# Moving three kinds of side work in a fused attention, mixture-of-experts and SwiGLU kernel: weight conversion, the first expert's sums, and the last expert's down products

## The chip, the cores and the metric

The kernel runs on one core of a Trainium2 chip. A time is the device time of one execution in microseconds (us). TensorE does the matrix products, VectorE (DVE in the profile) and ScalarE (ACT) the elementwise work, GpSimd (POOL) a few small steps and the DMAs that add into memory; SyncE (SP) issues nearly all the other DMAs.

## The reference

Attention with two mask kinds gives x of 2304 tokens by 512. A mixture of eight experts follows, and then a SwiGLU layer:

```
logits = x @ w_gate;  P = exp(logits - max)          # 2304 x 8
8 times: P /= row sums + 1e-9; P /= column sums + 1e-9; P *= 2304 / 8
out = 0
for e in range(8):
    out += P[:, e:e+1] * (relu(x @ w1[e]) @ w2[e])    # 512 -> 1024 -> 512
xn = out / sqrt(mean(out * out) + 1e-6) * rms_g
g = xn @ w_gate2;  result = (g * sigmoid(g) * (xn @ w_val)) @ w_out   # 512 -> 1536 -> 512
```

The weights of the last layer arrive as 64-bit floats; everything else is computed in 32-bit floats, each product as three products of rounded high and low parts.

## The kernel before

The tokens are three blocks (qd 0, 1, 2) of 768. Attention and expert 0 come first (to 329.1 us). Experts 1 to 7 are then 42 **groups**: for each expert g two halves hh of its hidden units, and for each half the three blocks, forwards for hh 0 and backwards for hh 1. Products of 2 by 2 blocks are done with 7 multiplications instead of 8, so operands have to be combined by adds before and outcomes after. A group has 14 up products (`product`, L1217, 84 matmuls) and 14 down units (`unit`, L1816, 126 matmuls), the units 12 slots behind: most of a group's units run in the next group. Both stream 32,256 columns. The last layer is nine **passes**: three thirds p of its hidden units, each for the three blocks (2, 1, 0, then 0, 1, 2, then 2, 1, 0). A pass is two **rounds** j of 14 up products and, from the second round on, the 36 down matmuls of the round before. In this document a stretch of the trace that is called a group or a round is cut at every 84th matmul of L1217.

The order of everything on each engine is the order in which this program issues it. `bg` is a clock that advances by one *pump* (28 in a group, about 1.07 us each; 26 in a round of the last layer); side work hangs on it as steps with a lag in pumps. `Queue` runs its steps in order, one lag after the other; a queue that yields waits while a rough model has VectorE too far behind TensorE (`room`, used only when `tight`). `drain` issues what is left of something at once.

The side work that the change touches:

- **Conversion** (`convert`, L817 to L862): 72 items turn 64-bit weights into 32-bit ones. An item is one load into `cv`, seven VectorE instructions (`head` 2, `number` 2, `tail` 2, `whole` 1) on 256 columns, one store. There is one buffer: the next `head` waits for its load, and, as it overwrites `t`, for the store before. 40 items (and 8 `first_combos`, which make the first third's up weights in memory) go from group 5 to group 39, where what is left is issued at once; the other 32 go from pass 1 on, in the queue `conv`. `load_1` and `prepare_2`, which bring the last layer's weights for the next third, call `conv.drain`: they issue every item up to the one they need.
- **Second weights** (`second_weights`, L1090): at each half's first group (n divisible by 3) seven combined blocks of w2 are made, by subtractions (L1106), rounding on ScalarE (L1119) and remainders on VectorE (L1122), all on 256 columns.
- **Sums of the experts.** `evict_1` takes a unit's outcome from PSUM to `acc` (copy on ScalarE, L1837, or add on VectorE, L1848); `close_region` weighs it with the expert's probability on ScalarE (L1867) and adds it to the memory tile `y1d` by a POOL DMA (L1873). Expert 1's two halves are added in `acc` and closed once, after hh 1. Expert 0's sums lie unweighted in `y0d`; in groups 2 to 5 `first_sums` loads each of 18 tiles to `cv`, weighs it (L1942) and stores it to `y1d` as the start of the sum.
- **Into the last layer.** After group 41 the loop `PRE_UNITS` runs 8 of the 12 units that are left, and pass 0's first products are interleaved with the other 4. `turn_tile` transposes normalized tiles (L1467, L1468) and queues `norm_blocks`, which splits and combines them (L1484 to L1506) and stores them to `xnd`; blocks of `xnd` are the passes' x operands. Block 0's tiles are turned in round (0, 1) (`TURNS`), and its downs are held back for that. Steps of `norm_blocks` have lags of 2.5, 1.6 and 0.85 pumps for blocks 0, 1 and 2. The up weights of round (0, 1) are loaded from `w1d` by `ready_combos`, queued at steps 1 and 3 of round (0, 0).

Of the kernel before, what the change touches and what calls it, by code (L numbers as in the profile page):

```python
# [17 lines left out]
P = 128  # L18
# [62 lines left out]
class Queue:  # L81


    def __init__(self, clock, yields=False, limit=8):
        self.clock = clock
        self.yields = yields
        self.limit = limit
        self.items = []
        self.last = 0
        clock.queues.append(self)  # L90
# [23 lines left out]
def kernel(  # L114
# [751 lines left out]
    def conversion(items, wait):  # L866

        for n, (nm, f, half) in enumerate(items):
            load, head, number, tail, whole, store = convert(nm, f, half)
            tag = nm, f  # L870
            if n == 0:
                conv.add([(WRITE, load)], tag)
            conv.add([(wait, head), (STEP, number), (STEP, tail)], tag)
            if n + 1 < len(items):
                conv.add([(STEP, whole), (1, convert(*items[n + 1])[0]), (2, store)], tag)
            else:
                conv.add([(STEP, whole), (WRITE, store)], tag)
# [212 lines left out]
    def second_weights(g, hh, both=None):  # L1090

        if both is None:
            both = const.tile([P, 2048], F32, name="raw_2", tag="r")
        raw = [both[:, 1024 * r : 1024 * (r + 1)] for r in range(2)]
        b11, b12, b21, b22 = ([t[:, 256 * i : 256 * (i + 1)] for t in raw] for i in range(4))
        new = [fa[:, 4608 + 256 * r : 4864 + 256 * r] for r in range(2)]
        t1, t3, t2, t4 = new, b12, b11, b21

        def load(r):
            f = 2 * hh + r  # L1100
            for h in range(2):
                rows = w2[g][(f + h * (NF // 2)) * P : (f + h * (NF // 2) + 1) * P, :]
                nc.sync.dma_start(out=raw[r][:, 512 * h : 512 * (h + 1)], in_=rows)

        def sub(out, a, b):
            nc.vector.tensor_tensor(out=out, in0=a, in1=b, op=ALU.subtract)  # L1106

        def early(r):
            sub(t1[r], b12[r], b11[r])
            sub(t3[r], b22[r], b12[r])  # L1110
            return 600

        def late(r):
# [7 lines left out]
        def low(k, r):  # L1121
            nc.vector.tensor_tensor(  # L1122
                out=w2_piece(k, r, 1), in0=(b21, b11, t4, t2, t1, t3, b22)[k][r],
                in1=w2_piece(k, r, 0).bitcast(F32), op=ALU.subtract,
            )
            return 256

        def begin():
            prep2.add([(WRITE, lambda: load(0)), (0, lambda: load(1))])

        def product(k):
            steps = []
            if k == 0:
                steps += [(READ, lambda: early(0)), (STEP, lambda: early(1))]
            steps += [(1, lambda: [high(k, r) for r in range(2)].clear()), (1, lambda: sum(low(k, r) for r in range(2)))]
            if k == 1:
                steps += [(1, lambda: late(0)), (1, lambda: late(1))]
            prep2.add(steps, ("w2", g, hh, k))

        return begin, product  # L1140
# [386 lines left out]
    with tc.manual_schedule():  # L1527
# [188 lines left out]
        for idx in range(-LOOK, n1 - LOOK):  # L1716
# [8 lines left out]
            if u.f == 0:  # L1725
                if "x" not in u.cell:
                    fetch(u)
                if u.left:
                    bg.add(gate(u.t0, u.n, u.cell["x"]), 20)
                    if u.at:  # L1730
                        area = fa[:, :1280], fa[:, 1280:3328].bitcast(F32R)
                        steps = sums(0, us[0].cell["x"], *area) if u.at == 1 else []
                        steps += sums(u.at, u.cell["x"], *area)
                        bg.add(steps, 30 if u.at == 1 else SUMS, tag="sums")
# [90 lines left out]
        def evict_1(n, k):  # L1825
# [9 lines left out]
            if (hh == 0 or E_STD < g < E - 1) and k in (0, 2, 3, 4):  # L1835
# [20 lines left out]
            if (hh == (g < E - 1) or E_STD < g < E - 1) and k in (1, 5, 6):  # L1856
                close_region(g, qd, *((1, 0) if k == 1 else (0, None) if k == 5 else (1, 1)))
# [3 lines left out]
        def close_region(g, qd, half, col):  # L1861
# [71 lines left out]
        def first_sums(i):  # L1933

            qd, b = divmod(i, 6)
            buf = cv[:, 512 * (i % 2) : 512 * (i % 2 + 1)]

            def load():
                nc.sync.dma_start(out=buf, in_=y0d[:, tile_of(qd, b), :])

            def weigh():
                nc.scalar.activation(buf, buf, AF.Copy, scale=prob[:, tile_of(qd, b), 0:1])  # L1942

            def store():
                nc.sync.dma_start(out=y1d[:, qd, b // 3, b % 3], in_=buf)

            return load, weigh, store
# [16 lines left out]
        for n, (g, hh, qd) in enumerate(groups):  # L1964
# [12 lines left out]
            if n == 2:  # L1977
                steps = []
                for i in range(17, -1, -2):
                    l, w, t = zip(first_sums(i), first_sums(i - 1))  # L1980
                    steps += [*l, lambda: None, *w, *t]
                bg.add(steps, 62, tag="first")
# [74 lines left out]
        ])  # L2057
        def downs(r):
# [46 lines left out]
        for n, (p, qd) in enumerate(passes):  # L2105
# [10 lines left out]
            if n == 1:  # L2116
                conv.yields = False
                conversion(conv_items[40:], CONV_WAIT[1])
            for j in range(NG // 2):
# [14 lines left out]
                for ci, s in enumerate((2 * j, 2 * j + 1)):  # L2134
# [8 lines left out]
                    for i, (wk, xk, which, begins) in enumerate(PROD):  # L2143
                        fetch_left(None)
                        if n < NQD and j == 0 and ci == 0:
                            for x in PROD[i : i + 3]:
# [6 lines left out]
                        if first_round:  # L2153
# [15 lines left out]
                        if step in late:  # L2169
                            if NGP - 1 not in spares:  # L2170
                                spares[NGP - 1] = spare_of(NGP - 1)
                            turn_tile(groups[-1][2], late[step], db[late[step] % 3], spares[NGP - 1])
# [48 lines left out]
```

## Time and profile before

| | |
|---|---|
| median of 3 runs | 2202.3 us (2201.37 to 2205.28) |
| the profiled execution | 2203.58 us, span of its instructions 2201.8 us |
| TensorE busy | 2045.3 us, 93% |
| VectorE, ScalarE, GpSimd busy | 1622.5, 1300.6, 246.2 us |
| mean granted TensorE clock | 0.975 of full speed |

The profile has for each stretch the busy time of each engine, the granted clock and how busy the DMA engines are; for each engine, what ended its idle times; and the single instructions in order of time. Busy time is a union: two instructions that overlap count once, so a group's busy time can be less than its count times the mean.

### The profile page before, as it was taken

The page shows a single profiled execution, that of the slowest core. Times are in us where ns is not written, and L with a number is a line of the kernel's source. Part 1 is how long each engine was busy: PE and PEld are TensorE (multiplying, and loading weights), DVE is VectorE, ACT ScalarE, POOL GpSimd, SP SyncE. Part 2 cuts the span into 40 slices and gives each one's busy share as a digit, 9 for nine tenths or more (in the row PEclk, how much of TensorE's full clock was granted, in tenths as well). Part 3 has the DMA queues.
Part 4 walks back from the last instruction along what each step waited for, and adds up shares of the span by engine and source line. Part 5 has one row for each costly group of instructions (what it writes and reads, how often), then busy time and mean ns, then how long its engine had stood idle before and what let it go on. Part 6 is the DMA issues. An engine that isn't in the chain of part 4 may idle for free. (4 is left out here: it accounts for less than half of the span.)

```text
span 2201.8 us, 37643 instructions
## 1 busy us (share of the span) xinstructions
PE 2045.3 (93%) x13611; PEld 1938.0 (88%) x13611; DVE 1622.5 (74%) x3553; ACT 1300.6 (59%) x2991; POOL 246.2 (11%) x277
## 2 busy tenths in 40 slices
PE   8999998999999999999999999999987889894798
PEld 7788878989999999999999999999987778794697
DVE  4667657869787887878878788787886557675644
ACT  6756335756776777777777777777664334231222
POOL 6433200000111011110111111111000000000000
PEclk9999999999999999999999999999999999997899
DMA  6687675676877879778897887976757662432431
GB/s 184 162 234 190 201 244 202 213 256 152 240 198 191 243 174 263 193 208 239 218 279 208 234 212 185 265 191 183 221 151 262 229 200 82 151 131 79 135 143 58
DMA packets 357146, 429.54 MB, mean 195 GB/s; under 512 B 80800, under 2 KB 260192, under 8 KB 356960
## 3 DMA queue, kind: packets, MB, share of 16 engines
q1 hardware_dynamic: 321888, 368.20, 51.6%
q0 software_dynamic: 35072, 58.93, 16.0%
q8 instruction: 108, 1.77, 0.3%
q14 instruction: 78, 0.64, 0.1%
HBM read 301.75 MB, written 125.30 MB: 194 GB/s over the span
## 5 line engine op out<-in xcount | busy, mean ns | idle before, releaser
L1217 PE MATMUL ub<-xt,w1t 128*128 128x384 f32 x2328 | 477.7, 342 | 30.6 <-DMA xt<-xnd 14.5
L1217 PE MATMUL ub<-xx,w1t 128*128 128x384 f32 x1956 | 398.7, 341 | 47.0 <-DVE fa L1249 30.4
L1217 PEld LDWEIGHTS ub<-xt,w1t 128*128 128x128 f32 x2328 | 401.7, 192 | 41.0 <-issue 11.2
L1816 PE MATMUL db<-w2t,ht 128*128 128x256 f32 x2772 | 383.5, 283 | 8.9 <-DVE acc L1848 5.7
L1217 PEld LDWEIGHTS ub<-xx,w1t 128*128 128x128 f32 x1956 | 336.0, 191 | 55.7 <-DVE fa L1249 32.8
L1816 PEld LDWEIGHTS db<-w2t,ht 128*128 128x128 f32 x2772 | 369.1, 190 | 13.4 <-DVE acc L1848 9.5
L1816 PE MATMUL db<-w2t,hx 128*128 128x256 f32 x2520 | 350.9, 284 | 8.0 <-DVE acc L1848 3.8
L1816 PEld LDWEIGHTS db<-w2t,hx 128*128 128x128 f32 x2520 | 334.7, 190 | 17.7 <-DVE acc L1848 12.5
L1249 DVE TENSOR_TENSOR fa<-ub,fa 128x384 f32<-128x384 f32 x360 | 199.5, 554 | 180.2 <-PE ub L1217 171.3
L1368 ACT ACTIVATE fa<-fa 128x384 f32<-128x384 f32 x252 | 132.2, 525 | 192.9 <-DVE fa L1249 192.3
L1873 POOL DMA_DIRECT2D y1d<-acc x99 | 114.2, 1153 | 1097.1 <-ACT acc L1867 475.8
L1245 DVE TENSOR_TENSOR ht<-fa,ht 128x384 fp32r<-128x384 f32 x344 | 189.5, 552 | 45.0 <-ACT ht L1242 44.3
L1245 DVE TENSOR_TENSOR hx<-fa,hx 128x384 fp32r<-128x384 f32 x316 | 174.4, 552 | 35.9 <-ACT hx L1242 34.8
L1242 ACT ACTIVATE ht<-fa 128x384 fp32r<-128x384 f32 x344 | 177.2, 518 | 32.6 <-DVE fa L1420 32.2
L1242 ACT ACTIVATE hx<-fa 128x384 fp32r<-128x384 f32 x316 | 162.4, 520 | 56.7 <-DVE fa L1420 55.2
L1323 DVE TENSOR_TENSOR fa<-fa 128x384 f32<-128x384 f32 x336 | 185.5, 552 | 5.2 <-ACT fa L1364 0.7
L1867 ACT ACTIVATE acc<-acc,prob 128x256 f32<-128x256 f32 (+1 forms) x324 | 176.0, 572 | 16.2 <-DVE acc L1848 16.1
L1848 DVE TENSOR_TENSOR acc<-db,acc 128x768 f32<-128x768 f32 (+1 forms) x129 | 154.4, 1197 | 39.9 <-PE db L1816 38.9
L1360 ACT COPY fa<-ub 128x384 f32<-128x384 f32 x252 | 119.6, 475 | 107.0 <-PE ub L1217 103.4
L1385 ACT COPY fa<-ub 128x384 f32<-128x384 f32 x108 | 51.7, 479 | 129.8 <-PE ub L1217 129.6
L1837 ACT COPY acc<-db 128x768 f32<-128x768 f32 x144 | 115.1, 800 | 20.6 <-PE db L1816 16.4
L1403 ACT ACTIVATE fa<-fa 128x384 f32<-128x384 f32 x54 | 28.3, 525 | 110.1 <-DVE fa L1249 110.1
(259 smaller groups left out, 3145.3 us busy)
## 6 DMA issues: line engine op xcount, KB each, us to landing
xt<-xdt SPq DMA_DIRECT2D x111, 768.0 KB
xx<-xdt SPq DMA_DIRECT2D x92, 768.0 KB
y1d<-acc POOLq DMA_DIRECT2D x66, 384.0 KB, 7.3
y1d<-acc POOLq DMA_DIRECT2D x33, 768.0 KB, 10.1
xt<-xnd SPq DMA_DIRECT2D x25, 768.0 KB
xx<-xnd SPq DMA_DIRECT2D x24, 768.0 KB
fa<-in_moe_w_dram SPq DMA_DIRECT2D x56, 256.0 KB
raw<-in_moe_w_dram SPq DMA_DIRECT2D x52, 256.0 KB
```

The costliest lines, as they stand in the source:

```text
L1217: nc.tensor.matmul(ps[:, :TH], w[i][:, c], x[:, k, c], start=first and c == 0 and n == 0, stop=c == 1 and n == 2, skip_group_check=True,)
L1242: nc.scalar.activation(h[0], src, func)
L1245: engine.tensor_tensor(out=h[1], in0=src, in1=h[0].bitcast(F32), op=ALU.subtract)
L1249: nc.vector.tensor_tensor(out=out, in0=ps, in1=more, op=ALU.add)
L1323: nc.vector.tensor_tensor(**kw)
L1360: nc.scalar.copy(z[nm], ps)
L1368: nc.scalar.activation(z[nm], z[nm], AF.Relu)
L1816: nc.tensor.matmul(spot(k, m), hm[x], w[y], start=BEGIN[k] and r == 0 and m in FIRST[PAIR[k]] and i == 0, stop=r == 1 and i == 2, skip_gro ...
L1837: nc.scalar.copy(a, ps)
L1848: nc.vector.tensor_tensor(out=a, in0=ps, in1=a, op=ALU.add)
L1867: nc.scalar.activation(a, a, AF.Copy, scale=prob[:, tile_of(qd, b), g : g + 1])
L1873: nc.gpsimd.dma_start(out=y, in_=t, accum_op=ALU.add)
```

## The change

- `Queue` gets `paused`; `conv` is paused in the groups with n divisible by 3 up to group 38. Conversion starts at group 2 instead of 5, its wait before a `head` is 6 pumps instead of 11; `first_combos` waits 6 instead of 8.
- From pass 1 on (`quick`) the wait is 4 instead of 6, other steps have a lag of 1, and the next load and the store follow `whole` at once.
- `second_weights` works on 512 columns at a time: half the instructions.
- Expert 1 is closed after each half like experts 2 to 6. The closings of half 0 whose probabilities are not ready yet wait in a list until group 2; the first one of a place in `y1d` writes instead of adding. Expert 0's tiles are loaded in groups 7, 10, 13, 16 and 19 (four at a time), weighed 9 to 15 pumps later and added to `y1d` by POOL DMAs.
- `PRE_UNITS` is 12. Block 0's tiles are turned at steps 7 to 12 of round (0, 0); round (0, 1) has the common order of downs. Lags of `norm_blocks` are 1.0, 1.0, 0.85. The `w1d` loads for round (0, 1) are issued together, before pass 0, and the first load for the next third is queued there.
- The steps of one early `sums` task in expert 0 are spaced unevenly.

```diff
     def pump(self):
-        while self.items and self.last + self.items[0][1] < self.clock.now and (not self.yields or len(self.items) > self.limit or self.clock.room()):
+        while self.items and not self.paused and self.last + self.items[0][1] < self.clock.now and (not self.yields or len(self.items) > self.limit or self.clock.room()):
...
-    CONV_WAIT = (11, 6)
-    PRE_WAIT = 8
-    PRE_UNITS = 8
+    CONV_WAIT = (6, 4)
+    PRE_WAIT = 6
+    PRE_UNITS = 12
...
-    BLOCK_LAG = (2.5, 1.6, 0.85)
-    TURNS = (2, 3, 4, 6, 7, 8), (1, 1, 2, 2, 3, 3, 4, 5, 6, 6, 8, 9, 10, 12)
+    BLOCK_LAG = (1.0, 1.0, 0.85)
+    LAST_TURN = (7, 8, 9, 10, 11, 12)
+    Y0_AT = (7, 10, 13, 16, 19)
...
-    def conversion(items, wait):
+    def conversion(items, wait, quick=False):
...
-            conv.add([(wait, head), (STEP, number), (STEP, tail)], tag)
+            step = 1 if quick else STEP
+            conv.add([(wait, head), (step, number), (step, tail)], tag)
             if n + 1 < len(items):
-                conv.add([(STEP, whole), (1, convert(*items[n + 1])[0]), (2, store)], tag)
+                conv.add([(step, whole), (0 if quick else 1, convert(*items[n + 1])[0])], tag)
+                conv.add([(0 if quick else 2, store)], tag)
...
-        def high(k, r):
-            nc.scalar.activation(w2_piece(k, r, 0), (b21, b11, t4, t2, t1, t3, b22)[k][r], AF.Copy)
+        def place(k, s):
+            return w2t[:, k].rearrange("p s n -> p (s n)").rearrange("p (r s n) -> p r s n", r=2, s=2)[:, :, s]
+
+        def high(k):
+            nc.scalar.activation(place(k, 0), (b21, b11, t4, t2, t1, t3, b22)[k], AF.Copy)
...
-            if (hh == 0 or E_STD < g < E - 1) and k in (0, 2, 3, 4):
+            if (hh == 0 or g < E - 1) and k in (0, 2, 3, 4):
...
-                bg.drain("first")
-                if g < E - 1:
+                if (g, hh) == (E_STD, 0):
+                    nc.gpsimd.dma_start(out=y, in_=t)
+                elif g < E - 1:
                     nc.gpsimd.dma_start(out=y, in_=t, accum_op=ALU.add)
...
+        def first_sums(tiles):
+
+            t = const.tile([P, 2048], F32, name="y0_r", tag="r").rearrange("p (i n) -> p i n", n=DM)
...
+            for i, (qd, b) in enumerate(tiles):
+                bg.later(0, lambda i=i, qd=qd, b=b: load(i, qd, b))
+                bg.later(9 + 2 * i, lambda i=i, qd=qd, b=b: (weigh(i, qd, b), add(i, qd, b)))
...
             if n == 2:
...
+                waiting_for, early = early, None
+                bg.add([lambda a=a: close_region(*a) for a in waiting_for], 12, bg.now + 8)
+            if n in Y0_AT:
+                i = 4 * Y0_AT.index(n)
+                first_sums([divmod(x, 6) for x in range(i, min(i + 4, NTILE))])
...
-            if n == 5:
-                bg.drain("first")
+            conv.paused = n % NQD == 0 and n < NGP - 3
+            if n == 2:
                 conversion(conv_items[:24], CONV_WAIT[0])
...
+        prep.drain(("w1", E, 1))
+        for j in (2, 3):
+            for part in range(1, 5):
+                ready_combos(E, j, part)
+        prep.add([(WRITE, lambda: load_1(E + 1, 0))])
...
-                conversion(conv_items[40:], CONV_WAIT[1])
+                conversion(conv_items[40:], CONV_WAIT[1], True)
...
-                            for x in PROD[i : i + 3]:
+                            for x in PROD[i : i + 4]:
...
-                            if step == 1:
-                                prepare_1(E, 2)
-                            if step == 3:
-                                prepare_1(E, 3)
+                            if step in LAST_TURN:
+                                t = LAST_TURN.index(step)
+                                if t == 0:
+                                    spares[NGP - 1] = spare_of(NGP - 1)
+                                turn_tile(groups[-1][2], t, db[t % 3], spares[NGP - 1])
```

## Rows read from the trace of the kernel before

**Rows 1.** The page: engines; two groups of instructions (busy, mean ns | idle before, releaser)

```profile
PE 2045.3 (93%) x13611; PEld 1938.0 (88%) x13611; DVE 1622.5 (74%) x3553; ACT 1300.6 (59%) x2991; POOL 246.2 (11%) x277
...
L1867 ACT ACTIVATE acc<-acc,prob 128x256 f32<-128x256 f32 (+1 forms) x324 | 176.0, 572 | 16.2 <-DVE acc L1848 16.1
L1848 DVE TENSOR_TENSOR acc<-db,acc 128x768 f32<-128x768 f32 (+1 forms) x129 | 154.4, 1197 | 39.9 <-PE db L1816 38.9
```

**Rows 2.** Busy time by stretch: groups 1 to 6, 7 to 40, rounds to 55

```profile
core 0: us, PE busy (x) PEld busy (x) DVE busy (x) ACT busy (x) POOL busy (x), PEclk, DMA share, GB/s
...
358.40:558.90 200.50, 188.12 (x1271) 183.62 (x1270) 160.05 (x336) 126.73 (x274) 9.19 (x8) 0.97 0.67 205
558.90:1602.60 1043.70, 1023.24 (x7143) 1006.56 (x7142) 854.80 (x1820) 770.25 (x1675) 116.27 (x101) 1.00 0.81 218
1602.60:2090.30 487.70, 398.12 (x2036) 361.88 (x2035) 331.93 (x770) 179.11 (x396) 4.61 (x5) 0.92 0.48 156
```

**Rows 3.** Busy time by stretch: single groups 4, 5, 6, 12, 14, 20

```profile
454.10:491.10 37.00, 32.72 (x213) 31.99 (x212) 21.56 (x36) 21.41 (x45) 2.28 (x2) 0.91 0.74 235
491.10:521.00 29.90, 29.85 (x213) 29.53 (x211) 27.16 (x53) 19.02 (x43) 3.45 (x3) 1.00 0.76 189
521.00:558.90 37.90, 33.77 (x213) 32.65 (x212) 35.07 (x79) 23.38 (x57) 3.45 (x3) 0.91 0.67 170
711.00:744.70 33.70, 31.00 (x212) 29.83 (x211) 32.03 (x76) 25.83 (x61) 3.45 (x3) 1.00 0.87 245
774.60:804.90 30.30, 29.80 (x212) 29.48 (x211) 25.62 (x56) 21.92 (x47) 3.45 (x3) 1.00 0.63 150
959.60:989.40 29.80, 29.80 (x212) 29.48 (x211) 25.20 (x54) 21.93 (x47) 3.45 (x3) 1.00 0.65 155
```

**Rows 4.** What ScalarE waited for in 458 to 476 us

```profile
ACT cv L1942 <- DMA cv<-y0d: 4.0, 2, 2.6
```

**Rows 5.** VectorE's groups of instructions in group 12 (711.0 to 744.7)

```profile
L1122 DVE TENSOR_TENSOR w2t<-raw,w2t 128x256 fp32r<-128x256 f32 x12 | 4.5, 418 | 0.4 <-ACT w2t L1119 0.4
...
L852 DVE SCALAR_TENSOR_TENSOR cv<-cv 128x256 f32<-128x256 uint32 x2 | 0.8, 425 | 0.1
```

**Rows 6.** Busy time by stretch, from group 41 on

```profile
1602.60:1663.40 60.80, 48.17 (x325) 46.57 (x323) 51.49 (x118) 32.97 (x77) 2.91 (x3) 0.92 0.58 182
1663.40:1724.20 60.80, 50.78 (x273) 45.92 (x274) 39.60 (x83) 28.55 (x67) 1.71 (x2) 0.94 0.78 249
1724.20:1819.20 95.00, 77.53 (x361) 68.79 (x360) 55.30 (x133) 34.63 (x77) 0.00 (x0) 0.91 0.60 196
1819.20:1992.60 173.40, 165.28 (x842) 150.39 (x841) 125.38 (x292) 62.93 (x134) 0.00 (x0) 0.99 0.35 120
1992.60:2090.30 97.70, 56.36 (x241) 50.21 (x240) 60.16 (x147) 20.04 (x43) 0.00 (x0) 0.77 0.32 105
2090.30:2114.80 24.50, 23.29 (x121) 21.33 (x121) 12.78 (x24) 6.91 (x15) 0.00 (x0) 1.00 0.28 106
2114.80:2137.80 23.00, 23.00 (x122) 21.38 (x121) 10.40 (x20) 6.93 (x15) 0.00 (x0) 1.00 0.54 190
```

**Rows 7.** What TensorE waited for in the whole span: total, times, longest

```profile
PE ub L1217 <- DVE fa L1249: 43.2, 17, 26.2
PE ub L1217 <- DMA xt<-xnd: 14.5, 3, 5.2
...
PE ub L1217 <- DMA w2t<-w1d: 5.9, 1, 5.9
...
PE ub L1217 <- DMA xx<-xnd: 5.0, 1, 5.0
```

**Rows 8.** VectorE's groups of instructions in 1992.6 to 2057.4

```profile
L2097 DVE TENSOR_TENSOR acc<-db,acc 128x512 f32<-128x512 f32 x5 | 3.4, 685 | 2.0 <-PE db L729 1.9
...
L834 DVE TENSOR_SCALAR cv<-cv 128x256 uint32<-128x256 uint32 x8 | 2.3, 293 | 15.5 <-DMA cv<-in_moe_w_val_dram 7.9 <-DMA cv<-in_moe_w_out_dram 7.7
```

**Rows 9.** SyncE's queue in order of time, 1729 to 1745 and 1999 to 2006

```profile
1730.64 0.47 SPq L826 DMA_DIRECT2D cv<-in_moe_w_out_dram  x1
...
2001.96 0.38 SPq L829 DMA_DIRECT2D cv<-in_moe_w_val_dram  x1
```

**Rows 10.** VectorE in order of time, the same two stretches

```profile
1739.53 0.29 DVE L834 TENSOR_SCALAR cv<-cv 128x256 uint32<-128x256 uint32 x1 [7.82 <-DMA cv<-in_moe_w_out_dram]
...
1999.74 0.29 DVE L834 TENSOR_SCALAR cv<-cv 128x256 uint32<-128x256 uint32 x1 [2.50 <-DMA cv<-in_moe_w_val_dram]
...
2001.97 0.42 DVE L858 TENSOR_TENSOR cv<-cv 128x256 f32<-128x256 f32 x1
2005.00 0.29 DVE L834 TENSOR_SCALAR cv<-cv 128x256 uint32<-128x256 uint32 x1 [2.61 <-DMA cv<-in_moe_w_val_dram]
```

More of the change, by code (lines that the diff above doesn't have):

```diff
@@ L89, in __init__ @@
         self.last = 0
+        self.paused = False
         clock.queues.append(self)
@@ L1093, in second_weights @@
             both = const.tile([P, 2048], F32, name="raw_2", tag="r")
-        raw = [both[:, 1024 * r : 1024 * (r + 1)] for r in range(2)]
-        b11, b12, b21, b22 = ([t[:, 256 * i : 256 * (i + 1)] for t in raw] for i in range(4))
-        new = [fa[:, 4608 + 256 * r : 4864 + 256 * r] for r in range(2)]
+        raw = both.rearrange("p (r n) -> p r n", r=2)
+        b11, b12, b21, b22 = (raw[:, :, 256 * i : 256 * (i + 1)] for i in range(4))
+        new = fa[:, 4608:5120].rearrange("p (r n) -> p r n", r=2)
         t1, t3, t2, t4 = new, b12, b11, b21
@@ L1133, in product @@
             if k == 0:
-                steps += [(READ, lambda: early(0)), (STEP, lambda: early(1))]
-            steps += [(1, lambda: [high(k, r) for r in range(2)].clear()), (1, lambda: sum(low(k, r) for r in range(2)))]
+                steps += [(READ, lambda: sub(t1, b12, b11)), (STEP, lambda: sub(t3, b22, b12))]
+            steps += [(1, lambda: high(k)), (1, lambda: low(k))]
             if k == 1:
-                steps += [(1, lambda: late(0)), (1, lambda: late(1))]
+                steps += [(1, lambda: sub(t2, b22, t1)), (1, lambda: sub(t4, b21, t2))]
             prep2.add(steps, ("w2", g, hh, k))
@@ L1733 @@
                         steps += sums(u.at, u.cell["x"], *area)
-                        bg.add(steps, 30 if u.at == 1 else SUMS, tag="sums")
+                        if u.at == 1:
+                            bg.add(steps, 30, tag="sums", weights=[0.8] * 9 + [1.0] + [2.0] * 4 + [0.8] * 6)
+                        else:
+                            bg.add(steps, SUMS, tag="sums")
                 else:
@@ L1855, in evict_1, with close_region @@
                     prepare_2(E, (0, 2, 1, 3)[k - 3])
-            if (hh == (g < E - 1) or E_STD < g < E - 1) and k in (1, 5, 6):
-                close_region(g, qd, *((1, 0) if k == 1 else (0, None) if k == 5 else (1, 1)))
+            if (hh == 0 or g < E - 1) and k in (1, 5, 6):
+                args = (g, hh, qd) + ((1, 0) if k == 1 else (0, None) if k == 5 else (1, 1))
+                if early is None:
+                    close_region(*args)
+                else:
+                    early.append(args)
             if (g, hh) == (E - 1, 1) and k >= 5:
                 scales[k - 5].add(norm_scale(qd, 3 * (k - 5)), ("scale", qd))
-        def close_region(g, qd, half, col):
+        early = []
+        def close_region(g, hh, qd, half, col):
             part = slice(0, DM) if col is None else slice(256 * col, 256 * (col + 1))
@@ L1931, in second, with load, weigh, add @@
             tick()
[L1933 to L1947, printed above, removed]
+        def first_sums(tiles):
+            t = const.tile([P, 2048], F32, name="y0_r", tag="r").rearrange("p (i n) -> p i n", n=DM)
+            def load(i, qd, b):
+                nc.sync.dma_start(out=t[:, i], in_=y0d[:, tile_of(qd, b), :])
+            def weigh(i, qd, b):
+                nc.scalar.activation(t[:, i], t[:, i], AF.Copy, scale=prob[:, tile_of(qd, b), 0:1])
+            def add(i, qd, b):
+                nc.gpsimd.dma_start(out=y1d[:, qd, b // 3, b % 3], in_=t[:, i], accum_op=ALU.add)
+            for i, (qd, b) in enumerate(tiles):
+                bg.later(0, lambda i=i, qd=qd, b=b: load(i, qd, b))
+                bg.later(9 + 2 * i, lambda i=i, qd=qd, b=b: (weigh(i, qd, b), add(i, qd, b)))
         def next_blocks(slots, was):
```

34 lines of the change are left out of this document (7 added, 27 removed).

## The prediction, made before the change was run

> **What bounds the kernel now.** I read the page first, then the busy times by stretch, then what each engine waited for where a stretch was too long, and last the order of instructions at those places. The page says that TensorE is busy 93% of the span and VectorE 74% [rows 1]; a change that removes no matmul can win only TensorE's idle and half-clock time. The stretches say where that is. A group without loss takes 29.9 us, as the stretches at 491.1 and 959.6 do [rows 3]. Groups 1 to 6 take 200.5 where six such make 179.4: 21.1 lost. Groups 7 to 40 take 1043.7 against 34 x 29.9 = 1016.6: 27.1 lost. [...]
>
> The waits name the causes: VectorE late with L1249 (43.2 us, 26.2 in one piece), x blocks from `xnd` late (14.5 + 5.0), up weights from `w1d` late (5.9) [rows 7].
>
> **Groups 1 to 6.** In group 4 ScalarE stands 4.0 us for expert 0's tiles from memory [rows 4]; it is the engine that frees the up products' PSUM, TensorE stops behind it, and the group takes 37.0 at a clock of 0.91 [rows 3]. The change takes those loads out of groups 2 to 5. Group 6 takes 37.9 with VectorE busy 35.07: it makes second weights, converts, and adds expert 1's outcomes. Conversion is paused there, and 4 of 7 adds of a block (12 in all, 1.2 us each [rows 1]) become ScalarE copies; it falls under the 27.16 that group 5 bears without loss. What comes in: 9 more closings, 27 instructions of 0.57 us [rows 1] on ScalarE, most crowded in group 2, where the list is worked off; ScalarE is busy 126.7 of 200.5 [rows 2], so this is covered; without the cover it would cost its 15 us less the 18 weighings that leave. Nine POOL DMAs come too; POOL is busy for 11% of the span [rows 1], and nothing here waits on it. Conversion from group 2 adds some 5 us of VectorE work a group where there was none. Of the 21.1 lost, 7.1 (group 4) and 8.0 (group 6) go, 2 come back: 13 won; bounds 8 and 18.
>
> **Groups 7 to 40.** The loss sits in groups divisible by 3: group 12 takes 33.7 with VectorE busy 32.03, groups 14 and 20 take 30.3 and 29.8 with 25.62 and 25.20 [rows 3]. Of group 12's 32.0 two conversions go: seven instructions take from 1999.74 to 2002.39, 2.65 us, on an otherwise free VectorE [rows 10], so about 4.8 by two. The halved second weights: 12 remainders on 256 columns take 4.5, 0.375 each [rows 5], a 512-column instruction takes 0.685 [rows 8], so a pair saves 0.065 and 11 pairs 0.7. That leaves 26.5, between groups 14 and 5, and those lost 0.4 and nothing. [...]
>
> The paused conversion has to fit into two groups of three. An item's lags sum to 13.5 pumps instead of 18.5, so 28 / 13.5 = 2.1 items fall to each open group instead of 1.5, +1.5 us of VectorE work: about 27 in a group like 14 or 20, what group 5 bears. Counting pumps, the 40 items and 8 combos end within group 38 as before they ended within 38; no burst at 39. Expert 0's 18 tiles: loaded four at a time in a group's first pump, weighed 9 to 15 pumps (10 to 16 us) later, so a load may take the 8.9 us of the slowest row below; the 18 adds replace 18 stores and go through POOL. At nothing; if late, ScalarE stops as in group 4, at most 7 us for each of five. A conversion's load has 8 pumps, 8.6 us, instead of 14 until its `head`. It takes 3.0 (issue 2001.96, `head` 2005.00) on a free queue and 8.9 (1730.64 to 1739.53) behind x blocks [rows 9, 10], so a bad one costs 0.3 and its clearance is gone: I allow 5. Of 27.1 lost 14 are won; bounds 5 and 22.
>
> **From group 41 on**, by stretch [rows 6]. A clean round takes 23.0, or 24.5 where VectorE takes the outcome of a pass.
>
> *1602.6 to 1663.4, group 41 and 8 units.* VectorE is busy 51.5 of 60.8: it is the limit. Four units come in (29.9 / 28 = 1.07 us each, 4.3) with their outcomes and the first blocks of block 1's normalization, some 4 us more for VectorE. They cover the wait for the first x block that ends this stretch (one of the three on `xt`, 14.5 in all [rows 7]). 60.8 becomes 65; bounds 61 and 70.
>
> *1663.4 to 1724.2, pass 0.* It loses the four units and the 5.9 for `w1d`. VectorE's 39.6 lose the units' outcomes and gain block 0's turning and blocks from later: about 45 in 14.6 + 23 of matmuls. The 20 `w1d` loads now pass SP in a row, at 0.4 us each [rows 9] 8 us, and behind them wait the stores to `xnd`, whose buffers ScalarE refills: between 0 and 8, I take 3. 60.8 becomes 50; bounds 42 and 60.
>
> *1724.2 to 1819.2, three rounds.* They hold 15 us of the waits for `xnd` [rows 7], all but the one above, and slow clock behind them. Blocks 1 and 0 are now normalized a round or more earlier: 27 steps at 1.0 pump instead of 1.6 and 2.5. Clean: 70. *1819.2 to 1992.6, seven rounds* lose little now; clean is 5 x 23.0 + 2 x 24.5 = 164. *1992.6 to 2090.3, pass 6* takes 97.7 where 47.5 would be clean: conversion has fallen behind, the third third's weights drain it, and VectorE, through which every second product leaves PSUM, stands another 15.5 us for the loads [rows 8]. In quick form an item takes 7 pumps, 52 pumps a pass, so all 32 end in pass 5, and this goes to 49.
>
> The price lies in the rounds before. Per item VectorE's 2.65 us are only moved: the whole stretch has 331.9 busy [rows 2] and would have 413 to do it in. But a load now has 4 pumps, 3.5 us, until VectorE wants it. On a free queue 3.0 suffice. At 1730.64, behind x blocks, it took 8.9 and VectorE stood 7.82 [rows 9, 10]. A 5.4 us stop for each of the passes 1, 3 and 4, at whose ends x blocks are loaded, is 16: 75 for the three rounds (bounds 70 and 86), 174 for the seven (164 and 190).
>
> Sum: 65 + 50 + 75 + 174 + 49 = 413, 74.7 less than 487.7.
>
> **In all** 13 + 14 + 75 = 102 of the profiled execution's 2203.6, 1.3 above the median: 2100. The early `sums` steps are only respaced; 0, with 2 either way.
>
> **Rivals.**
>
> *A, the forecast,* 2100, 2075 to 2125: chance 0.55.
>
> *B, loads late.* VectorE stops at both loads that meet x blocks in a pass, and pass 0 has its 8 us behind SP: 16 + 5, and up to the same again from clock lost behind stops. 2125 to 2170, typically 2135; 0.2. [...] Against it: the DMA engines are 0.35 busy in the seven rounds [rows 6].
>
> *C, everything hides:* conversion's loads arrive in time and pass 0 runs at its matmuls' pace: 16 + 10 less, and middle losses at their lower bounds, 2045 to 2075; 0.17. Against it: VectorE at 85% in the first stretch.
>
> *D, slower.* Every quick load takes 8.9 us. Then 32 x 5.4 = 173 us of stops stand against 118 won without any; it decides from 3.7 us a stop, a mean latency of 7.2. The DMA share of 0.35 speaks against it, 0.60 in the three rounds for it. 2215 or more; 0.04.
>
> *E,* the conversion only moves VectorE's overload forward, so that pass 6's gain is lost in passes 1 to 4: 2150 to 2200; 0.04, half of it within 0.2% of before, which is about what a measurement of this kernel can tell from no change.
>
> Faster by over 0.2%: 0.94; within: 0.02; slower: 0.04. The range takes A, most of B and the upper part of C: 2064 to 2145.
>
> **What would show it.** Right: groups divisible by 3 at 30 to 30.5 us with VectorE near 27; no wait for `y0d` on ScalarE in groups 2 to 5; pass 6 under 52 us with no conversion in it; no wait for `xnd` over 1 us in passes 1 and 2. Wrong: VectorE idle at L834 for over 30 us in passes 1 to 5; pass 0 over 60 us; waits for `y0_r` on ScalarE in groups 7 to 19.

## The result, and the profile after

The changed kernel takes 2122.9 us (median of 4, 2121.6 to 2127.5) against 2201.8 (2199.3 to 2205.3): a ratio of 0.9644, 95% interval 0.9624 to 0.9664, so 79 us less. The forecast was 2100, in a range of 2064 to 2145. The profiled execution has a span of 2124.7 where before's had 2201.8. Every time and ratio here and below is of fast runs; one execution of the run e3_early, of 3260 us at a granted clock of 0.555, is left out. Cut at the same matmuls as before (us):

| stretch | before | forecast | after |
|---|---|---|---|
| start to group 1 | 358.4 | 358.4 | 352.4 |
| groups 1 to 6 | 200.5 | 187.5 | 185.2 |
| groups 7 to 40 | 1043.7 | 1029.7 | 1029.7 |
| group 41 and the units behind it | 60.8 | 65 | 62.7 |
| pass 0 (two rounds) | 60.8 | 50 | 72.1 |
| three rounds | 95.0 | 75 | 83.9 |
| seven rounds | 173.4 | 174 | 179.8 |
| pass 6 | 97.7 | 49 | 48.0 |
| the rest | 111.5 | 111.5 | 110.9 |

In the groups and in pass 6 the totals are near the forecast. Pass 0 is the miss: it was to get 11 shorter and got 11 longer.

First the busy times by stretch of the kernel after: groups 1 to 6, groups 7 to 40, and among them groups 4, 5, 6, 11 and 12, which answer to [rows 2, 3].

```profile
core 0: us, PE busy (x) PEld busy (x) DVE busy (x) ACT busy (x) POOL busy (x), PEclk, DMA share, GB/s
445.90:477.90 32.00, 30.14 (x213) 29.62 (x212) 21.72 (x48) 21.25 (x44) 3.02 (x3) 1.00 0.73 237
477.90:507.80 29.90, 29.90 (x213) 29.58 (x212) 25.93 (x58) 22.18 (x48) 3.45 (x3) 1.00 0.75 185
507.80:537.60 29.80, 29.80 (x211) 29.48 (x211) 27.50 (x52) 25.14 (x54) 3.48 (x3) 1.00 0.79 203
...
659.40:691.60 32.20, 30.45 (x212) 29.71 (x211) 25.44 (x56) 21.60 (x47) 3.45 (x3) 1.00 0.62 149
691.60:721.50 29.90, 29.90 (x213) 29.58 (x212) 27.65 (x52) 25.59 (x54) 3.45 (x3) 1.00 0.93 268
...
352.40:537.60 185.20, 180.80 (x1270) 178.04 (x1269) 154.74 (x327) 135.27 (x281) 15.57 (x17) 1.00 0.66 203
537.60:1567.30 1029.70, 1018.79 (x7143) 1005.58 (x7142) 836.19 (x1674) 774.24 (x1616) 131.97 (x119) 1.00 0.84 228
```

Groups 6 and 12 now hold VectorE at 27.5 and TensorE does not stop in them. Group 4 is 5 us shorter. Group 11 (659.4 to 691.6) is longer: it took 29.9 before, with VectorE busy 23.62. It is not alone. The eleven groups of this stretch that are divisible by 3 went from 352.6 to 329.5 in all, 23.1 won; the other 23 went from 691.1 to 700.2, 9.1 lost. What VectorE waited for at the two instructions of conversion's `head` in groups 7 to 40 (busy, mean ns | idle before, releaser), first in before, then in after:

```profile
L835 DVE TENSOR_SCALAR cv<-cv 128x256 f32<-128x256 f32 x37 | 10.9, 294 | 1.3
L834 DVE TENSOR_SCALAR cv<-cv 128x256 uint32<-128x256 uint32 x37 | 10.6, 286 | 1.4 <-DMA cv<-in_moe_w_gate_dram 1.4
```

```profile
L837 DVE TENSOR_SCALAR cv<-cv 128x256 f32<-128x256 f32 x33 | 9.7, 294 | 9.6 <-DMA m2g<-cv 7.2 <-DMA m2v<-cv 1.1 <-DMA m2o<-cv 0.3
L836 DVE TENSOR_SCALAR cv<-cv 128x256 uint32<-128x256 uint32 x33 | 9.6, 290 | 5.3 <-DMA cv<-in_moe_w_val_dram 2.5 <-DMA cv<-in_moe_w_out_dram 1.9 <-DMA cv<-in_moe_w_gate_dram 0.9
```

The first instruction waits for the item's load, 5.3 us instead of 1.4, and the second for the store of the item before, 9.6 instead of 1.3; in group 11 this is 3.2 us at one store. That these waits cost the other groups their 9.1 us is argued from the trace: no run gives the loads and stores there more time. Then the same view from group 41 on; it answers to [rows 6].

```profile
1567.30:1630.00 62.70, 54.70 (x369) 53.20 (x368) 55.82 (x127) 34.02 (x79) 2.91 (x3) 0.89 0.60 194
1630.00:1674.00 44.00, 22.45 (x110) 20.71 (x109) 21.64 (x48) 18.30 (x44) 1.70 (x2) 0.77 0.85 262
1674.00:1702.10 28.10, 24.45 (x123) 20.91 (x121) 20.81 (x48) 12.85 (x32) 0.00 (x0) 1.00 0.75 222
1702.10:1786.00 83.90, 75.64 (x360) 67.55 (x361) 57.32 (x143) 29.27 (x61) 0.00 (x0) 0.94 0.58 196
1786.00:1965.80 179.80, 167.94 (x842) 150.02 (x841) 142.60 (x344) 64.64 (x139) 0.00 (x0) 0.99 0.39 134
1965.80:2013.80 48.00, 46.19 (x241) 42.69 (x240) 32.33 (x65) 19.62 (x43) 0.00 (x0) 1.00 0.32 113
```

In the first round of pass 0 (second row) TensorE is busy for half of 44.0 us at a granted clock of 0.77, and VectorE and ScalarE are busy for half as well: no compute engine is the bound, something is waited for. What TensorE and then ScalarE waited for in that round (us in total, times, longest):

```profile
PE ub L1215 <- DVE fa L1404: 14.0, 1, 14.0
PE ub L1215 <- ACT fa L1383: 5.5, 1, 5.5
```

```profile
ACT acc L1482 <- DMA xnd<-acc: 12.8, 1, 12.8
ACT w2t L1083 <- PE ub L1215: 6.1, 1, 6.1
```

And SP's order of issue there (start, us):

```profile
1618.94 1.09 SPq L1080 DMA_DIRECT2D fa<-m2o  x1
...
1633.67 0.33 SPq L1080 DMA_DIRECT2D fa<-m2o  x1
1634.06 8.24 SPq L938 DMA_DIRECT2D w1t<-w1d  x16
...
1646.51 2.20 SPq L938 DMA_DIRECT2D last_r<-w1d  x1
...
1653.89 0.90 SPq L938 DMA_DIRECT2D w2t<-w1d  x2
1654.90 1.73 SPq L1516 DMA_DIRECT2D xnd<-acc  x3
```

Read backwards from the 14.0: TensorE waits for VectorE's `L1404`, which stands behind a remainder of the normalization (`L1483`), which waits for ScalarE's rounding (`L1482`), which waits for its buffer, which the stores to `xnd` at 1654.90 have to empty. Those stores stand on SP behind not 20 but 36 loads of `w1d`, which hold SP from 1634.06 until the first of these stores at 1654.90: 20.8 us. The first 16 are those of regions 0 and 1, put into a paced queue in group 41 and forced out by the `prep.drain` that the change added; ahead of them stands the second `m2o` load, which waits for its buffer until 1633.67. The first `m2o` load, issued at 1618.94 behind seven x blocks, lets ScalarE's `L1083` start only at 1632.29; that is the 5.5. (The row above names TensorE as what ended ScalarE's wait. The traces of e2_pool and e3_early name the load, and e5_m2o, below, settles it.)

### The profile page after: what moved, and what is told of

Its sections match the earlier page's. It is cut to its first block, busy times and chain, and to the rows that moved or that the text cites. A ratio compares the mean times of both kernels' runs of the same rounds, so it can differ in the third digit from the quotient of the medians.

```text
span 2124.7 us, 37479 instructions
## 1 busy us (share of the span) xinstructions
PE 2027.7 (95%) x13611; PEld 1926.7 (91%) x13611; DVE 1594.4 (75%) x3387; ACT 1312.5 (62%) x2932; POOL 268.4 (13%) x304
## 5 line engine op out<-in xcount | busy, mean ns | idle before, releaser
L1366 ACT ACTIVATE fa<-fa 128x384 f32<-128x384 f32 x252 | 132.3, 525 | 180.6 <-DVE fa L1247 180.3
L1240 ACT ACTIVATE ht<-fa 128x384 fp32r<-128x384 f32 x344 | 177.4, 518 | 37.9 <-DVE fa L1418 37.4
L1874 ACT ACTIVATE acc<-acc,prob 128x256 f32<-128x256 f32 (+1 forms) x351 | 190.8, 573 | 14.3 <-DVE acc L1849 14.0
L1849 DVE TENSOR_TENSOR acc<-db,acc 128x768 f32<-128x768 f32 (+1 forms) x117 | 143.0, 1222 | 33.3 <-PE db L1817 32.1
L1838 ACT COPY acc<-db 128x768 f32<-128x768 f32 x156 | 124.5, 798 | 19.8 <-PE db L1817 16.8
L1383 ACT COPY fa<-ub 128x384 f32<-128x384 f32 x108 | 51.4, 477 | 92.0 <-PE ub L1215 91.8
L981 DVE TENSOR_TENSOR w1t<-fa,w1t 128x256 fp32r<-128x256 f32 (+1 forms) x160 | 83.4, 525 | 11.1 <-ACT w1t L978 10.7
```

The source lines that it names most:

```text
L1240: nc.scalar.activation(h[0], src, func)
L1366: nc.scalar.activation(z[nm], z[nm], AF.Relu)
L1838: nc.scalar.copy(a, ps)
L1849: nc.vector.tensor_tensor(out=a, in0=ps, in1=a, op=ALU.add)
L1874: nc.scalar.activation(a, a, AF.Copy, scale=prob[:, tile_of(qd, b), g : g + 1])
```

## The experiments

All edits begin from the changed kernel. Ratios are to the kernel before on the same chip. For pass 0 the theory, T, is that SP's order makes it long; its rivals are V, VectorE's normalization work, and D, the bytes on the DMA engines.

### The loads' place: e1_spread, e2_pool, e3_early

e1_spread:

```diff
-        prep.drain(("w1", E, 1))
-        for j in (2, 3):
-            for part in range(1, 5):
-                ready_combos(E, j, part)
-        prep.add([(WRITE, lambda: load_1(E + 1, 0))])
...
+                            if step in (1, 3):
+                                prepare_1(E, 2 + step // 2)
```

> One part of the change is undone in the changed kernel: the 20 w1d loads for regions 2 and 3 go back into the paced queue at steps 1 and 3 of the first round; all else stays. Theory T (SP's order: 36 loads in a row keep the xnd stores waiting for 12.9 us, and so ScalarE, VectorE and TensorE): the stores of the last six tiles issue behind 16 loads instead of 36, some 11 us earlier; TensorE's 14.0 us gap at L1215 shrinks to 0-5, the first round falls from 44 to 30-36, the time from 2123 to 2107-2114. Rival V (VectorE's work of pass 0, six norm turns and their blocks beside a round, is the bound): the first round stays over 40, the time within 4 of 2123. Rival D (the loads' bytes on the DMA engines, not their issue): the stores issue early but land as late as before, gain under 5.

e2_pool:

```diff
-                nc.sync.dma_start(
+                (nc.gpsimd if j > 1 else nc.sync).dma_start(
                     out=at(7 * i + k, n).bitcast(F32).rearrange("p (k m) -> p k m", k=n),
```

> The 20 w1d loads for regions 2 and 3 are issued at the same place in the program, but by GpSimd instead of SP; all else as in the changed kernel. T: as the loads no longer stand ahead of the stores on SP, the stores issue some 11 us earlier; 14.0 us gap to 0-6, time 2107-2115. D (bytes on the DMA engines): the loads move just as many bytes at the same time, so the xnd stores and the x loads behind them land late all the same; gap over 9, time 2118-2124. V: within 4 of 2123.

e3_early:

```diff
                         prepare_1(*nxt, PARTS_AT[i])
+                        if n + 1 == NGP:
+                            prep.drain(("w1", E, r))
```

> The w1d loads for regions 0 and 1 (20) are issued in group 41 right behind the product that ends their region's use, not from a queue that yields to VectorE; so 16 of them no longer stand behind the second m2o load and ahead of the 20 loads and the stores. All else as in the changed kernel. T: the xnd stores issue some 8 us earlier, the 14.0 us gap falls to 4-8, and the 5.5 us gap at the start of the round, in which the product waits, goes if it is the w1d loads and stays if it is ScalarE's wait for the m2o load; time 2107-2116. V: within 4 of 2123.

Ratios 0.9641 (0.9614 to 0.9668), 0.9654 (0.9638 to 0.9670) and 0.9648 (0.9615 to 0.9680). None differs from 0.9644 by what the intervals can tell, so I read the traces by round. The two rounds of pass 0 in e1_spread, in e2_pool, and in e3_early:

```profile
1633.70:1664.00 30.30, 21.02 (x111) 18.45 (x110) 21.58 (x48) 18.18 (x44) 1.70 (x2) 0.89 0.95 291
1664.00:1699.40 35.40, 28.16 (x122) 24.23 (x121) 21.32 (x48) 12.99 (x32) 0.00 (x0) 0.87 0.92 286
```

```profile
1630.00:1672.30 42.30, 24.42 (x111) 22.40 (x110) 21.65 (x48) 18.41 (x44) 12.51 (x22) 0.76 0.88 289
1672.30:1700.60 28.30, 24.40 (x122) 20.87 (x120) 20.83 (x48) 12.89 (x32) 0.00 (x0) 1.00 0.74 220
```

```profile
1626.80:1663.10 36.30, 23.56 (x110) 21.83 (x109) 21.65 (x48) 18.30 (x44) 1.70 (x2) 0.76 0.87 264
1663.10:1691.00 27.90, 24.45 (x122) 20.91 (x121) 20.84 (x48) 12.90 (x32) 0.00 (x0) 1.00 0.76 226
```

V falls: the first round can take 30.3 with the same VectorE work (21.6). T is half right. In e1_spread the 14.0 us wait is gone and the first round is 13.7 shorter, but the second takes 7.3 more, with the DMA engines at 0.92. In e3_early the wait falls to 4.1 and pass 0 from 72.1 to 64.2; but this edit moves the bytes of 16 loads out of the round as well as their place on SP, and does not tell T from D. e2_pool does, in part. Its first round starts at 1630.0 as after's does. The stores issue on SP at 1644.77, ten us earlier, and ScalarE goes on at 1653.33 instead of 1658.80: 5.5 of the ten us reach it. So SP's order is part of the wait, and D fits the rest: with GpSimd issuing the loads, the stores had an earlier start, and half of it was lost again, in a round with the DMA engines 0.88 busy. TensorE still stops 6.7 and 6.6, and the round gains only 1.7, but this edit has a price of its own: GpSimd's step of the normalization (`L1455`) now stands behind the 20 loads. What ScalarE waited for in that round of e2_pool:

```profile
ACT acc L1482 <- DMA xnd<-acc: 5.6, 1, 5.6
...
ACT acc L1458 <- POOL cv L1455: 3.0, 1, 3.0
```

### Both together, and the m2o load: e4_both, e5_m2o, e6_all

e4_both is e1_spread with e3_early. e5_m2o is e3_early and

```diff
-        prep2.add([(WRITE, load), (READ, high), (STEP, low)], ("w2", i))
+        prep2.add([(WRITE, load), (14 if (g, f) == (E, 0) else READ, high), (STEP, low)], ("w2", i))
```

e6_all is all three.

> Both of the earlier edits in the changed kernel: the w1d loads of regions 0 and 1 issue in group 41 (as in e3_early), those of regions 2 and 3 go back into the paced queue of the first round (as in e1_spread). In single executions e3_early won 8 us over pass 0's two rounds (72.1 to 64.2), e1_spread 6 (the first round 44.0 to 30.3, the second 28.1 to 35.4). If SP's order alone held pass 0 (T), both add up: first round 28-31, second 28-31, pass 0 56-62, time 2107-2113. If the DMA engines' bytes hold it (D; they are 0.85 to 0.95 busy in all first rounds so far), the second edit only shifts the loads from the first round to the second: pass 0 63-66, time as e3_early or 1-2 more.

> e3_early, and ScalarE's first copy of the m2o weights comes 14 pumps after its load instead of 7. In after and e3_early ScalarE stands some 6 to 7 us at that copy, as the load lands 13 us after its issue behind seven x loads, and TensorE's 5.5 to 6.6 us gap at L1215 <- ACT L1383 follows. If that copy is the cause, the gap falls under 2 and pass 0 from 64 to 57-60, time 5-7 under e3_early's. Rival: the product waits for its x block or w1t in any case, the gap moves to another releaser and the time is within 2 of e3_early's.

> e4_both and e5_m2o's later copy together. T: first round near 25, second near 30, time 2102-2109. D: as e5_m2o within 2.

Ratios 0.9638 (0.9614 to 0.9662), 0.9604 (0.9582 to 0.9626), 0.9613 (0.9592 to 0.9635); medians 2122.9, 2112.6, 2117.1. Pass 0 in e4_both, in e5_m2o, and in e6_all:

```profile
1632.30:1663.20 30.90, 20.63 (x110) 18.52 (x109) 21.58 (x48) 18.19 (x44) 1.70 (x2) 0.89 0.79 235
1663.20:1696.80 33.60, 27.45 (x122) 23.20 (x120) 20.79 (x48) 12.89 (x32) 0.00 (x0) 0.90 0.87 269
```

```profile
1626.40:1658.50 32.10, 21.75 (x110) 19.52 (x109) 20.93 (x47) 17.10 (x41) 1.70 (x2) 0.84 0.93 294
1658.50:1687.10 28.60, 25.80 (x123) 22.55 (x121) 20.78 (x48) 13.01 (x32) 0.00 (x0) 0.94 0.73 217
```

```profile
1635.50:1661.30 25.80, 20.42 (x110) 18.33 (x109) 20.84 (x47) 17.03 (x41) 1.70 (x2) 0.93 0.89 269
1661.30:1696.30 35.00, 27.30 (x123) 23.61 (x121) 20.84 (x48) 12.98 (x32) 0.00 (x0) 0.90 0.83 257
```

Pass 0 takes 64.5, 60.7 and 60.8. Spreading the loads adds nothing once the first 16 are early (64.5 against e3_early's 64.2, 60.8 against 60.7): it gives time to the first round and takes it from the second, as D has it. It is no proof of D: in the second round SP issues nine of the spread loads right ahead of stores (1676.70 to 1681.85 in e1_spread), so that T could do the same. T's forecast for e6_all, 2102 to 2109, did not come. The later copy of `m2o` takes the wait at `L1383` from 6.6 to 2.1 and 3.5 off pass 0. So the changed kernel's pass 0 was 72.1 through the place of the first 16 loads (8) and the `m2o` copy (3.5); at 60.7 it is back to what it took before. These are single executions, but others agree: the five runs u1 to u5 below leave pass 0 alone and have it at 72 to 75, and e8_wait5, which has e5_m2o's edits, at 59. e5_m2o is faster than the changed kernel: the ratios differ by 0.0040, about 9 us, with about 0.0030 for the uncertainty of that difference.

What holds it at 60 is argued only. Pass 0 of e5_m2o moves 32.1 x 294 + 28.6 x 217 = 15.6 MB; at the higher of the two rates, at which the DMA engines are 0.93 busy, that is 53 us. No run took bytes away.

### The last layer's conversion: u1_plain, e8_wait5

u1_plain:

```diff
-                conversion(conv_items[40:], CONV_WAIT[1], True)
+                conversion(conv_items[40:], 6)
```

> The quick conversion of the last 24 half pieces is undone in the changed kernel: pace 6 and step 1.5 as before, pieces in their old order of issue; the conversion again ends in pass 6. Prediction's term: pass 6 goes from 48 back to 97 (+49), passes 1 to 5 lose their conversion stops (some 16 us by the prediction; 20 us of VectorE idle time at conversion loads in the trace of after, most of it hidden): time 2123+30 to 2123+45 = 2153-2168. Rival E (overload only moved forward): under +15.

Ratio 0.9831 (0.9811 to 0.9851), 2164.6: the quick form is worth 41 us. Its stretches: the three rounds, the seven, and pass 6.

```profile
1704.10:1782.60 78.50, 72.52 (x360) 65.14 (x361) 47.61 (x112) 30.29 (x64) 0.00 (x0) 0.98 0.52 183
1782.60:1955.80 173.20, 164.79 (x841) 150.46 (x840) 125.58 (x291) 63.90 (x136) 0.00 (x0) 0.99 0.36 121
1955.80:2053.40 97.60, 56.61 (x241) 50.71 (x240) 60.57 (x149) 19.74 (x43) 0.00 (x0) 0.77 0.33 107
```

Pass 6 is as before, 97.6 against 48.0: 49.6 won there, 5.4 and 6.6 paid in the rounds ahead. The prediction paid 16. The prediction's rival E, that what pass 6 gains is lost again ahead of it, is out.

e8_wait5 is e5_m2o with `CONV_WAIT = (6, 5)` in place of `(6, 4)`.

> e5_m2o (2112.6) with the last layer's conversion at a pace of 5 pumps instead of 4 until a piece's first step. u1_plain shows that quick conversion costs rounds 44 to 53 some 12 us. If these are waits for the pieces' loads, as the prediction has them (4 pumps, 3.5 us, against loads of 3.0 to 8.9), one pump more saves 3 to 7: 2106-2110. If it is VectorE's work that delays the outcomes, nothing changes: 2111-2114. If the conversion then ends too late for the last third's weights, pass 6 is over 50 and the time over 2115.

Ratio 0.9619 (0.9602 to 0.9635), median 2111.7: no different from e5_m2o's 0.9604. By stretch its trace is 5.0 and 3.4 shorter in the ten rounds (80.2 for 85.2, 177.3 for 180.7), as the loads theory asks, and pass 6 stays at 48.2; but up to group 41 that execution was 8.7 longer than e5_m2o's, in places that the edit does not touch. The median lies where the expectation had put VectorE's work as the cause (2111 to 2114), not where it had put the loads (2106 to 2110). VectorE's idle time at `L836` falls only from 19.0 to 16.1. That one pump more helps the rounds is shown in one trace, not in the time.

### One part undone: u5_weights, u2_pairs, u3_nopause, u4_adds

u5_weights takes `weights=[0.8] * 9 + [1.0] + [2.0] * 4 + [0.8] * 6` out of the first sums.

> One part undone in the changed kernel: the steps of the first two sums tasks are spaced evenly again, all else stays. My prediction had 0 +-2 for it; from the start to group 1 the trace of after is 6.0 us shorter (352.4 against 358.4), and the 3.8 us stop with a half-clock stretch at 122.9 is gone. If the spacing is the cause, the time goes up by 4 to 8 (2127-2131) and group 1 starts near 358; if the 6 us come from elsewhere (expert 0's last outcomes or the scatter of single executions, 318 to 323 at group 0), it stays within 2.

Ratio 0.9705 (0.9684 to 0.9726), 13 us; by spans 7.8, of which 5.4 ahead of group 1 (357.8 against 352.4). The twelve traces with uneven spacing, after's among them, reach group 1 at 348.9 to 353.8. What TensorE waited for from 110 to 135 us, and ScalarE from 90 to 135, in u5_weights; the trace of after has no such waits:

```profile
PE ps_p L555 <- DVE lsm L510: 3.5, 1, 3.5
```

```profile
ACT fa L1183 <- DMA xdt<-fa: 9.2, 1, 9.2
```

From 120 to 130 us the granted clock is 0.66 in u5_weights, as it is before, and 1.00 in after. So the spacing does it. With even spacing a rounding of the sums on ScalarE (`L1183`) stands 9.2 us (9.5 in before) for stores to `xdt` that still read its buffer; VectorE stands 6.9 us behind ScalarE at `L765`, the attention's softmax (`L510`) comes after that, TensorE stops for 3.5 us, and its clock falls to the 0.66.

u2_pairs puts the old `second_weights` back, two halves of 256 columns for each instruction of 512.

> One part undone in the changed kernel: the second weights are again made in halves of 256 columns, 22 VectorE instructions a region where the changed kernel has 11. [...] The time per group tells less: if the groups divisible by 3 keep their slack (27.6 busy of 29.9 in groups 6 and 12), the time rises by 0 to 4; a forecast by VectorE's busy time alone would be +9 to +22.

Ratio 0.9736 (0.9716 to 0.9755): 20 us, not 0 to 4. Group 12 (692.6 to 723.4) and groups 7 to 40 of u2_pairs, and then VectorE's instructions of the second weights in that stretch (busy us, mean ns), first of u2_pairs, then of after:

```profile
692.60:723.40 30.80, 30.39 (x213) 29.67 (x212) 28.64 (x63) 25.97 (x61) 3.45 (x3) 1.00 0.91 249
...
536.90:1581.30 1044.40, 1025.60 (x7143) 1008.29 (x7142) 847.90 (x1795) 779.18 (x1693) 132.00 (x119) 1.00 0.84 225
```

```profile
L1126 DVE TENSOR_TENSOR w2t<-raw,w2t 128x256 fp32r<-128x256 f32 x132 | 49.6, 417 | 4.1 <-ACT w2t L1123 4.0
L1110 DVE TENSOR_TENSOR raw<-raw 128x256 f32<-128x256 f32 x44 | 18.7, 425 | 1.5
```

```profile
L1120 DVE TENSOR_TENSOR w2t<-raw,w2t 128x512 fp32r<-128x512 f32 x66 | 45.1, 684 | 5.9 <-ACT w2t L1117 5.9
L1110 DVE TENSOR_TENSOR raw<-raw 128x512 f32<-128x512 f32 x22 | 15.1, 685 | 0.1
```

A remainder's pair saves (49.6 - 45.1) / 66 = 0.068, my 0.065; a subtraction's saves (18.7 - 15.1) / 22 = 0.164. Over the stretch VectorE is busy 11.7 less with 121 fewer instructions, 0.097 each. The expectation's +9 is 13 regions at my 0.7; at 0.097 their 143 pairs make 14, and no run shows its +22. What it does to the time is not in these figures: 1 us more of VectorE in group 12, 28.64 for 27.65, makes it 0.9 longer. There was no slack at 27.6. The eleven groups divisible by 3 are 9.3 longer together. The rest of the 14.7 lies in the other groups, whose sum differs by up to 8 us between traces of kernels that are alike there.

u3_nopause sets `conv.paused = False`.

> One part undone in the changed kernel: conversion is no longer paused in the groups divisible by 3; its pace of 6 stays. By the prediction two conversions, 4.8 us, come back to each of these groups: VectorE goes from 27.6 to some 32 there and the 11 groups from 29.9 to 31-33; the other groups get emptier and conversion ends some ten groups earlier. Time +8 to +25. Rival: VectorE's idle time covers it (27.6 + 4.8 is 32.4 against 29.9, but the surplus spreads into the next groups with 25-27), time within 4.

Ratio 0.9793 (0.9776 to 0.9809): 33 us, over the 25 that I set as the upper end. Group 6 and groups 7 to 40 of it:

```profile
506.50:538.70 32.20, 30.34 (x212) 29.68 (x211) 30.76 (x64) 25.12 (x54) 3.48 (x3) 1.00 0.90 242
...
538.70:1589.70 1051.00, 1025.97 (x7142) 1009.79 (x7141) 830.78 (x1650) 773.89 (x1616) 131.84 (x119) 1.00 0.83 222
```

VectorE's work in groups 7 to 40 is 5 us less than in after (830.78 for 836.19), and they take 21.3 longer, 15.9 of it in the eleven groups divisible by 3: it is where the work stands that counts, not how much it is.

u4_adds makes expert 1's second half add in VectorE again:

```diff
-            if (hh == 0 or g < E - 1) and k in (0, 2, 3, 4):
+            if (hh == 0 or E_STD < g < E - 1) and k in (0, 2, 3, 4):
```

with the closings of expert 1's first half left out and its second half stored as it is.

> One part undone in the changed kernel: expert 1's second half is again added to its first in VectorE (four outcomes of a block, 12 adds, go from ScalarE copies to VectorE adds in groups 4 to 6), and it is closed once; expert 0's tiles still come from groups 7 to 19 on. By the prediction group 6's 8.0 us came from the pause and these copies together, group 4's 7.1 from the tiles' loads alone: VectorE in groups 4 to 6 goes from 75.2 to some 89, the time up by 3 to 8. Rival: as group 6 has 27.5 busy of 29.8 and conversion makes way when VectorE is behind, under 2.

Ratio 0.9707 (0.9684 to 0.9730), 14 us, over the 8 that I set as the upper end. Its profiled execution was the shortest of its four by 9 us and does not show them. Groups 5 and 6:

```profile
472.80:503.40 30.60, 29.96 (x212) 29.58 (x211) 29.11 (x62) 18.80 (x43) 2.11 (x3) 1.00 0.58 207
503.40:535.20 31.80, 30.67 (x213) 29.86 (x212) 30.89 (x56) 22.66 (x50) 2.11 (x3) 1.00 0.53 176
```

VectorE has 60.00 in these two instead of 53.43, and they are 2.7 longer, while group 4 is 2.1 shorter. Where the other ten go stays open.

The parts undone cost 13, 20, 33, 14 and 41 us, 121 together: more than the 79 won, and more than the 90 won outside pass 0. Three of them take VectorE's work out of groups 5 and 6 or out of those divisible by 3, so each one undone may be enough to put such a group over its limit; no run undoes two of them together, and this stays argued. No run undoes the move of expert 0's tiles or the earlier normalization either: what these are worth is read from the stretches alone.

## Why the prediction came near, point by point

*Start to group 1.* Not priced but for the sums, at 0 with 2 either way: wrong, 6.0 won, which for the total was luck. u5_weights shows the spacing as the cause. Before's trace had the stop at `lsm`, 3.8 us, and the half-clock stretch, 0.50 from 122 to 126 us, and I had not looked at that stage.

*Groups 1 to 6:* 15.3 for 13. Group 4 fell from 37.0 to 32.0, not to 29.9: VectorE stands 4.0 us in it at `L837`, for the store of the item before. Group 6 fell from 37.9 to 29.8 as said. Group 3 gave 3 us that the sum does not have; in before ScalarE stood 4.0 us for expert 0's tiles there too. ScalarE waits for none of expert 0's tiles there, nor for `y0_r` in groups 7 to 19.

*Groups 7 to 40:* 14.0 for 14, but by two errors that cancel, so the agreement is luck. The mechanism was right: groups divisible by 3 take 29.9 at 27.6 of VectorE, and gave 23.1. What I had the other groups pay was too small. I charged 5 for conversion's tighter loads; VectorE stands 5.3 for them at `L836`, in three stops. The sum has no term for the other wait of `head`, for the store of the item before: 9.6 at `L837`. These groups lost 9.1. Eleven traces of kernels alike in groups 7 to 40 take 1029.7 to 1037.5 there, and after's is one of the two shortest; the groups divisible by 3 take 329.5 in each. Two small sums are off without effect: two conversions of 2.65 us are 5.3, not 4.8, and by its lags a load had 13 pumps before, not 14. The pairs save 1.1 us a region (7 x 0.068 + 4 x 0.159, from all forms) instead of my 0.7. That the margin is so thin was in no step: group 5 bearing 27.16 said nothing of 28.6.

*Group 41 and the units:* 62.7 for 65.

*Pass 0:* 72.1 for 50. The step that failed is the one for SP: "The 20 `w1d` loads now pass SP in a row, at 0.4 us each [rows 9] 8 us, and behind them wait the stores to `xnd`, whose buffers ScalarE refills: between 0 and 8, I take 3." The place and the chain were right, the size was not: 36 loads hold SP for 20.8 us, 0.58 each, and the wait is 12.8 on ScalarE and 14.0 on TensorE. The drain ahead of the loop forces out 16 loads more, which a yielding queue had kept. Two things were missing beside it: the first `m2o` load behind seven x blocks, and a bound for the bytes. My 14.6 + 23 us of matmuls and VectorE's 45 never asked what the DMA engines move in the time, although before's first round had them 0.92 busy, which the 0.78 for the whole pass in [rows 6] does not show:

```profile
1663.40:1688.70 25.30, 22.77 (x129) 21.04 (x129) 17.59 (x38) 17.08 (x40) 1.71 (x2) 0.93 0.92 299
```

*Three and seven rounds:* 83.9 for 75, 179.8 for 174. Undone, the quick conversion gives back 5.4 and 6.6, less than my 16. What was too small is what I called clean: without it (u1_plain) the rounds take 78.5 and 173.2, not 70 and 164. So the first sum failed by its base, and the second came near because a charge of 11 for 6.6 made up for part of it. VectorE stands 17.8 us for `L836`'s loads in the ten rounds, in 12 pieces of at most 3.7; I had expected three of 5.4. The first of these rounds takes 33.0 by itself (1702.1 to 1735.1); a wait of 4.1 us of VectorE at `L1498` for an `xnd` store lies in it, which I had said would not be.

*Pass 6:* 48.0 for 49, and no conversion in it: its list of VectorE's instructions holds none on `cv`.

Of the prediction's rivals, B named the place that went wrong, the loads in a row on SP, but with 8 us of SP's time where they took 20.8. C, D and E did not come.

## What to carry to other kernels

Count the issues that a drain forces out, not those in the loop that one reads, and ask which store stands behind them on the same queue (in pass 0 36 issues, not 20, and 20.8 us ahead of the stores); then ask what the DMA engines can move in the stage (they were 0.79 to 0.95 busy in the first rounds of pass 0), before a sum over the compute engines is believed. An engine that is idle for a fifth of its time on the average, as VectorE is in groups 7 to 40, can be at its limit in every third group: here 1 us taken out of such a group was worth 0.9 us (group 12 of u2_pairs), and 3.3 us moved to its neighbours 2.4 (group 6 of u3_nopause). Who moves work with a load and a store in it to a tighter pace should price the wait for the store (9.6 us in groups 7 to 40) as well as that for the load (5.3). And a load issued behind large ones should have its reader put off: here one ScalarE copy that stood 7.1 us for its load (e3_early) held up all that came behind it on that engine.

## What was not expected of the hardware

The 36 `w1d` loads of pass 0 held SP for 0.58 us each on the mean (20.8 us), the time between them included. Most single ones took 0.32 to 0.43 us, like the loads to `cv` from which my 0.4 came [rows 9], and one took 2.2. The `m2o` load issued behind seven x blocks reached its reader 13.3 us later (1618.94 to 1632.29); the trace of after puts ScalarE's wait for it down to TensorE, those of e2_pool and e3_early to the load itself (7.1 us). In u2_pairs two neighbouring remainders of 256 columns overlap: two take 0.75 us, one 0.42. Two neighbouring subtractions, of which the second reads or overwrites what the first one wrote or read, have 0.03 us between them. So a pair costs 0.068 over one instruction of 512 for the remainders, and 0.164 for the subtractions.
